# Unit outputs behind the next unit's chain: a recurrence in chunks feeding a routed MoE

## The chip, the cores and the metric

The kernel runs on one core of a Trainium2 chip. The metric is the device time of one execution in microseconds (us). Engines are named as in the profile: PE is the matrix engine (PEld its weight loads), DVE the vector engine, ACT the scalar engine, POOL GpSimd, SP the queue that issues most DMAs.

## The reference

```python
for t in range(S):                                  # S=768, B=4, H=8, D=40
    y[:, :, t] = einsum('bhd,bhde->bhe', r_t, state)
    Sa = einsum('bhde,bhe->bhd', state, a_t)
    state = state*w_t[:, :, None, :] - einsum('bhd,bhe->bhde', Sa, b_t) \
            + einsum('bhd,bhe->bhde', v_t, k_t)
x = y.transpose(0, 2, 1, 3).reshape(B*S, H*D)       # N=3072 tokens of 320
logits = x @ w_gate + log1p(exp(x @ w_noise)) * noise
# two largest logits of each token, softmax over the two -> top2, top2_w
out[mask_e] += top2_w * (relu(x @ w1[e]) @ w2[e])   # 8 experts, hidden 1024
```

A linear recurrence with a 40x40 state for each of 32 heads, and behind it a mixture of 8 experts of which every token takes two.

## The kernel before

**Units.** The sequence is cut into 12 chunks of 64 steps and the batches into two pairs, which gives 24 units n = 0 to 23; unit n works on chunk n//2 and pair n%2. Its chain needs the state that unit n-2 left (`Sst`, one per pair). Four units make a group; there are six groups.

**Preparing a group.** While group w runs, group w+2 is prepared. `prepA` makes the decayed factors (on DVE: the scan `Gx`, then `NH`, `raww`, `NG_`, `nge`, `rawba`, `gm`, `pk`), once per batch pair, behind the state updates of units 4w and 4w+2. They go to DRAM and come back as PE operands (`d_ab`, `st_ab`). `scoresL`, called in iterations 4w+1 and 4w+3, makes the scores: `psc<-st_ab` on PE (two blocks of 16 matmuls for one batch pair), `lt` and `lo` on ACT, `scr` to DRAM on SP. When both pairs are there, `tsolve` loads all of the group's triangles at once (`X<-scr` on SP, one buffer), solves them in 30 pairs of steps (`Tt<-X`, L582, and `X<-X,Tt`, L583) on DVE for groups 0 and 1 and on POOL for groups 2 to 5, and stores the result (`scr<-X`). `fetchB` brings it back for each unit as `T` (`T<-scr`, on POOL's queue).

**A unit.** Its pieces on PE: the *chain*: `pW<-sE` (state times operand), `pQ<-w,T` (first apply, 64 matmul rows in the trace), `pW<-q,lo`, `pQ<-w,T` again (second apply, 32 rows), then `pS`, which ends in DVE's new `Sst` (L686). PE and ACT alternate in it: `w<-pW` and `q<-pQ` are copies on ACT. *pre* makes the next unit's `psc<-st_ab,st_k`, `ak` on DVE and `pW<-Vz,ak`. *outp*, the output: `pu` turns `Ut` (copied to `uT` on DVE), two halves of `psc<-RV(,uT)` through a single PSUM buffer, each taken out by DVE as `P` (L699), `pd` turns the state (`sD`, one buffer), `pY<-sD,RV`, `pY<-kb,P`, `pgm`, and DVE's product `xt` (L709). *Logits*: `xd<-xt` to DRAM, `px<-idm,xt`, `xT`, `pl`, then some 40 short operations on DVE and ACT, and *placing* (`drain`, one unit later: the one-hots `ohA`, `ohB`, then `pn<-ohB,ohA`), which counts the tokens of each expert.

**Order.** The order on every engine is written out by the tile scheduler at build time, from the program's order and priorities: the chain has a high priority (`PRIO=1500`), everything else stands where the program puts it and moves up where its inputs and buffers allow. A matmul burst runs through the helper at L470 (transposes L471), so their line says nothing; the tile names do.

**Experts.** After the last unit the tokens are sorted, gathered and put through the experts (`ph` L287, `po` L309).

Of the kernel before, what the change touches and what calls it, by code (L numbers as in the profile page):

```python
# [8 lines left out]
F32 = mybir.dt.float32  # L9
# [11 lines left out]
NA=20  # L21
# [382 lines left out]
class Att:  # L404
    PSC=1; PACC=3; PT=2; PPB=1
    def __init__(s,nc,tc,ctx,aps):
        s.nc,s.tc,s.aps=nc,tc,aps
        ec=ctx.enter_context
        s.inp=ec(tc.tile_pool(name="inp",bufs=1))
        s.tmp=ec(tc.tile_pool(name="tmp",bufs=1))  # L410
        o=sorted(range(SAB),key=lambda i:(i-12)%SAB); s.sab={i:ec(tc.tile_pool(name=f"sab{i}",bufs=1)) for i in o}
        s.stk=ec(tc.tile_pool(name="stk",bufs=1))
        s.wk=ec(tc.tile_pool(name="wk",bufs=2))
        s.cp=ec(tc.tile_pool(name="cp",bufs=1))
        s.late=ec(tc.tile_pool(name="late",bufs=1))
        s.dr=ec(tc.tile_pool(name="dr",bufs=2,space=DRAM))
        s.psa=ec(tc.tile_pool(name="psa",bufs=1,space=PSUM)); s.psb=ec(tc.tile_pool(name="psb",bufs=1,space=PSUM)); s.ps=ec(tc.tile_pool(name="ps",bufs=1,space=PSUM))
        s.consts()
    def consts(s):
        nc=s.nc; t=s.cp.tile  # L420
        nc.scalar.preload_act_table_set("natural_log_exp_and_others")
        s.d1=t([120,NS,65],F16,name="d1"); nc.vector.memset(s.d1,0.0); nc.vector.memset(s.d1[:,:,0:1],1.0)
        s.idf=t([128,128],F32,name="idf"); nc.gpsimd.memset(s.idf,1.0)
        nc.gpsimd.affine_select(out=s.idf,in_=s.idf,pattern=[[1,128]],base=0,channel_multiplier=-1,compare_op=ALU.is_equal,fill=0.0)
        s.ids=t([128,128],F16,name="ids"); nc.vector.tensor_scalar_mul(s.ids,s.idf,SC)
# [172 lines left out]
    def fetchR(s,o,cc):  # L598

        nc=s.nc; n,p=o['n'],o['G']['p']  # L600
        vt=s.aps[1][p,cc]; o['vu']=s.stk.tile([128,2,8,40],F32,name="vu",bufs=VUB)
        nc.sync.dma_start(o['vu'][0:64].rearrange("p b h e->p b (h e)"),vt.rearrange("(b s) x->s b x",b=2))
        rv=s.RV[n%2]
        for j in range(2): nc.sync.dma_start(rv[64*j:64*j+48,j:j+2].rearrange("p x i b t->p (x i b t)"),s.aps[3][p,cc,j])
        o['v'],o['r'],o['rr']=rv[:,1],[rv[:,0],rv[:,2]],rv[:,0::2]
# [45 lines left out]
    def turned(s,p):  # L651

        pd=s.ps.tile([128,4,2,64],F32,name="pd",tag="pt",bufs=s.PT)
        s.burst([s.tp(pd[:,i].rearrange("p b e->p (b e)"),s.Sst[p][:,2*i:2*i+2].rearrange("p h d->p (h d)"),s.idf) for i in range(4)])
        sD=s.wk.tile([128,4,2,40],F32,name="sD",bufs=1)
        s.copy(ESD,sD,pd[...,0:40])
        return sD
    def chain(s,p,cc,o):
# [28 lines left out]
        return sD  # L687
    def outp(s,o,sD,xout):
        nc=s.nc; kb=o['kb']
# [5 lines left out]
        for b in range(2):  # L695
            pp=s.psa.tile([128,4,2,64],F32,name="psc",tag="psc",bufs=s.PSC)
            s.burst([s.mm(pp[64*j:64*j+64,i],x[:,i,b],o['rr'][:,:,i,b],start=True,stop=True) for i in range(4) for j,x in ((1,uT),(0,o['v']))])
            m=s.wk.tile([128,8,64],F32,name="P",bufs=2)
            nc.vector.tensor_tensor(m,pp.rearrange("p i j t->p (i j) t"),s.mk.to_broadcast([128,8,64]),op=ALU.mult)  # L699
            P.append(m)  # L700
        Y=s.psb.tile([128,8,64],F32,name="pY",tag="pacc",bufs=s.PACC)
        if sD is not None:
# [8 lines left out]
    def run(s,m,xo=None):  # L711
# [11 lines left out]
        def idx(n): g,q=divmod(n,4); c,p=divmod(q,2); return g,c,p,g*CG+c  # L723
# [3 lines left out]
        def fR(n):  # L727
            if n<N: s.fetchR(O[n],idx(n)[3])
        def O_(n): g,c,p,cc=idx(n); return O.get(n) or {'G':grp[g][p],'c':c}
        def fB(n):  # L730
# [5 lines left out]
        s.prepC(grp[0][0],gate)  # L736
        with after(s.sl.ins): fA(0); fR(0)
        s.prepC(grp[0][1],gate)
        with after(s.sl.ins): fA(1); fR(1)
        s.pre(O[0]); s.blocks(O[0])  # L740
# [3 lines left out]
        if m is not None:  # L744
            with after(xd),(ExitStack() if 0 in MG else after(pl)): m.consts2(s.dm.bitcast(F32))
        xts=[]; aD=None; rA,rC={},{}
        for n in range(N):
# [19 lines left out]
            if q%2 and (gn if q==1 else gn+1)<NG:  # L767
                z=(gn,1) if q==1 else (gn+1,0)
                with behind(n-1): rA[z]=s.loadA(z[1],z[0])
            aD=s.aD  # L770
            if n+1<N: s.pre(O[n+1])
            xt=s.wk.tile([128,360],F32,name="xt",bufs=2)
            s.outp(O[n],sD,xt); xt=xt[:,0:DM]
            if n+1<N: s.blocks(O[n+1])
            fA(n+2); fR(n+2)
            if m is not None:
                m.drain(1)
                if n==NA+1: m.drain(); m.turn()
                m.logits(2*cc+p,xt,s.ps,("pt","pp"),(s.PT,s.PPB))
                if ZN<=n<ZN+4:  # L780
                    with after(m.xw.ins): m.zero(n-ZN)
            else: nc.sync.dma_start(xo[p,cc],xt)
LA=7; LC=4; RB=3
# [19 lines left out]
ZN=12  # L803
# [98 lines left out]
def build(nc,tc,A,out):  # L902
    with ExitStack() as ctx:
        m=Moe(nc,tc,ctx,(A['wgn'],A['nz'],A['w1'],A['w2'],out))
        with ExitStack() as c2:
            s=Att(nc,tc,c2,(A['fm'],A['vt'],A['fm2'],A['rv']))
            m.burst=s.burst; s.run(m)
            m.flag(s.ps,"pt",s.PT,s.mags)
# [28 lines left out]
```

## Time and profile before

| | us |
|---|---|
| median of 3 runs | 997.6 (996.33 to 1008.94) |
| profiled execution | 1001.79, its span 999.9 |
| PE busy | 800.1 (80%) |
| DVE busy | 555.8 (56%) |
| ACT busy | 392.1 (39%) |
| POOL busy | 349.6 (35%) |

The span is what the trace shows of the profiled execution; the rest of its time lies around the span. All positions in the trace are microseconds from the span's start, and all rows come from this one execution. The units run from about 90 to 577 us, the experts from there to the end.

### The profile page before, as it was taken

The page shows a single profiled execution, that of the slowest core. Times are in us where ns is not written, and L with a number is a line of the kernel's source. Part 1 is how long each engine was busy: PE and PEld are TensorE (multiplying, and loading weights), DVE is VectorE, ACT ScalarE, POOL GpSimd, SP SyncE. Part 2 cuts the span into 40 slices and gives each one's busy share as a digit, 9 for nine tenths or more (in the row PEclk, how much of TensorE's full clock was granted, in tenths as well). Part 3 has the DMA queues.
Part 4 walks back from the last instruction along what each step waited for, and adds up shares of the span by engine and source line. Part 5 has one row for each costly group of instructions (what it writes and reads, how often), then busy time and mean ns, then how long its engine had stood idle before and what let it go on. Part 6 is the DMA issues. An engine that isn't in the chain of part 4 may idle for free.

```text
span 999.9 us, 27350 instructions
## 1 busy us (share of the span) xinstructions
PE 800.1 (80%) x11706; PEld 701.9 (70%) x11706; DVE 555.8 (56%) x1198; ACT 392.1 (39%) x820; POOL 349.6 (35%) x477
## 2 busy tenths in 40 slices
PE   0123556888885988898788689999999999999995
PEld 0113455767764767676667478899999999999995
DVE  9358658857489687447357471643444444443430
ACT  2202343355453355353335232543434444343421
POOL 6000000149449429629500105416060707070403
PEclk9999957697797999999988799999999999999998
DMA  4794888586785957973553204507070706161303
GB/s 117 188 230 111 223 216 219 138 232 156 185 251 123 239 154 189 270 197 91 140 159 118 69 8 86 171 13 195 7 195 8 191 11 187 16 178 25 37 7 40
DMA packets 102022, 134.72 MB, mean 135 GB/s; under 512 B 37232, under 2 KB 82996, under 8 KB 100852
## 3 DMA queue, kind: packets, MB, share of 16 engines
q1 hardware_dynamic: 90100, 110.60, 41.1%
q0 software_dynamic: 11792, 22.29, 11.1%
q8 instruction: 94, 1.54, 0.7%
q14 instruction: 36, 0.29, 0.1%
HBM read 96.25 MB, written 39.88 MB: 136 GB/s over the span
## 4 chain that ended last, share of the span: by engine, by line
PE 54%; DVE 13%; DMA 11%; POOL 9%; issue 6%; ACT 3%; SPq 2%; POOLq 0%; ACTq 0%; DVEq 0%
PE ph L287 19%; PE po L309 17%; POOL X L583 4%; POOL Tt L582 4%; PE psc L470 3%; PE pY L470 2%; PE pt L268 2%; PE pW L470 2%; DMA T<-scr 2%; DVE X L583 2%; PE pQ L470 2%; DVE Tt L582 2%; DMA X<-scr 2%; DMA d_ab<-pk 1%; DMA scr<-X 1%
## 5 line engine op out<-in xcount | busy, mean ns | idle before, releaser
L311 POOL DMA_INDIRECT out_dram<-y,oi x56 | 94.2, 1682 | 227.1 <-ACT y L310 214.9
L290 DVE SCALAR_TENSOR_TENSOR hl<-ph,hh 128x256 fp32r<-128x256 f32 (+1 forms) x128 | 71.1, 557 | 132.3 <-ACT hh L288 131.8
L288 ACT ACTIVATE hh<-ph 128x320 fp32r<-128x320 f32 (+1 forms) x128 | 66.0, 519 | 151.8 <-PE ph L287 150.4
L470 PE MATMUL pQ<-w,T 32*32 32x40 f32 x2304 | 44.4, 214 | 47.7 <-DMA T<-scr 33.8
L583 POOL TENSOR_TENSOR X<-X,Tt 128x30 f32<-128x30 f32 (+14 forms) x120 | 78.1, 651 | 8.8
L470 PEld LDWEIGHTS pQ<-w,T 32*32 32x32 f32 x2304 | 37.7, 119 | 58.4 <-issue 38.5
L252 POOL DMA_INDIRECT xr<-xd,gi x56 | 54.8, 979 | 61.7 <-DVE dv L177 28.2
L309 PE MATMUL po<-w2h,hh 128*128 128x320 f32 x384 | 74.2, 313 | 0.6 <-ACT hh L288 0.6
L582 POOL TENSOR_TENSOR Tt<-X 128x30 f32<-128x30 f32 (+14 forms) x120 | 71.5, 596 | 8.5
L309 PE MATMUL po<-w2h,hl 128*128 128x320 f32 x384 | 70.8, 311 | 0.0
L287 PE MATMUL ph<-xh,w1h 128*128 128x512 f32 (+1 forms) x256 | 69.4, 355 | 1.0 <-DVE hl L290 1.0
L287 PE MATMUL ph<-xh,w1l 128*128 128x512 f32 (+1 forms) x256 | 68.9, 350 | 0.0
L287 PE MATMUL ph<-xl,w1h 128*128 128x512 f32 (+1 forms) x256 | 68.6, 349 | 0.0
L699 DVE TENSOR_TENSOR P<-psc,mk 128x512 f32<-128x512 f32 x48 | 33.0, 687 | 63.3 <-PE psc L470 63.3
L470 PE MATMUL psc<-RV,uT 128*64 128x128 f32 x384 | 61.5, 309 | 7.0 <-DVE P L699 4.8
L309 PE MATMUL po<-w2l,hh 128*128 128x320 f32 x384 | 65.7, 309 | 0.0
L585 POOL DMA_DIRECT2D scr<-X x5 | 3.2, 648 | 173.7 <-DVE X L583 172.5
L309 PEld LDWEIGHTS po<-w2h,hh 128*128 128x128 f32 x384 | 61.0, 188 | 3.4 <-ACT hh L288 0.8
L470 PE MATMUL psc<-RV 128*64 128x128 f32 x384 | 61.5, 309 | 1.2 <-issue 1.1
L470 PEld LDWEIGHTS <-st_ab 120*64 120x64 f16 (+1 forms) x928 | 28.6, 122 | 45.1 <-issue 28.6
L309 PEld LDWEIGHTS po<-w2h,hl 128*128 128x128 f32 x384 | 59.8, 188 | 0.5
L470 PEld LDWEIGHTS psc<-RV,uT 128*64 128x64 f32 x384 | 47.8, 155 | 15.7 <-DVE P L699 6.5
(315 smaller groups left out, 1927.6 us busy)
## 6 DMA issues: line engine op xcount, KB each, us to landing
w2r<-in_w_dram SPq DMA_DIRECT2D x8, 1280.0 KB
RV<-in_rv_dram SPq DMA_DIRECT2D x48, 192.0 KB
rawba<-in_fm_dram SPq DMA_DIRECT2D x24, 360.0 KB
d_ab<-pk SPq DMA_DIRECT2D x24, 360.0 KB
st_ab<-d_ab SPq DMA_DIRECT2D x12, 720.0 KB
w1r<-in_w_dram SPq DMA_DIRECT2D x8, 1024.0 KB
raww<-in_fm_dram SPq DMA_DIRECT2D x12, 365.6 KB
st_ab<-d_ab SPq DMA_DIRECT2D x24, 180.0 KB
```

Source lines behind the costliest of these rows:

```text
L252: k=t//128; nc.gpsimd.indirect_dma_start(out=X[:p,k if s.cap==CAP else 0],out_offset=None,in_=s.xd[int(w is not s.early[0])],in_offset=OFF ...
L268: for t,p in tiles(t0,n): nc.tensor.transpose(pt[:,t-t0:t-t0+p],x[:p,t//128,f0:f0+128],s.idm[:p,:p])
L287: for i,(a,b) in enumerate(mm): nc.tensor.matmul(ph[:,:n],a,b,start=i==0,stop=i==7)
L288: nc.scalar.activation(hh[:,f,:n],ph[:,:n],AF.Relu)
L290: if c.stop>c.start: nc.vector.scalar_tensor_tensor(o,ph[:,c],0.0,hh[:,f,c].bitcast(F32),op0=ALU.max,op1=ALU.subtract)
L309: s.lm=nc.tensor.matmul(po[:p],h[:,f,r],w[:,f],start=k==0,stop=k==23); k+=1
L311: st=nc.gpsimd.indirect_dma_start(out=s.out_d,out_offset=OFFS(ap=idx[:p,e,ii:ii+1],axis=0),in_=y[:p],in_offset=None,compute_op=ALU.add)
L470: def mm(s,*a,**k): return lambda: s.nc.tensor.matmul(*a,**k)
L582: eng.tensor_tensor(t,Xt[:,j:j+1,j+1:].to_broadcast([128,j,m]),Xt[:,0:j,j:j+1].to_broadcast([128,j,m]),op=ALU.mult)
L583: s.tl=eng.tensor_tensor(Xt[:,0:j,j+1:],Xt[:,0:j,j+1:],t,op=ALU.add)
L585: q.dma_start(scr2.rearrange("g c h i j x->(g c h i) (j x)"),Xt.rearrange("p j t->p (j t)"))
L699: nc.vector.tensor_tensor(m,pp.rearrange("p i j t->p (i j) t"),s.mk.to_broadcast([128,8,64]),op=ALU.mult)
```

## The change

`outp` is cut in two. The new `outp` keeps `pu`, `uT`, the two `psc<-RV` halves and `P`; the rest (`pY`, `pgm`, `xt`) is `outq`. A new function `finish(n)` holds `outq`, the store of `xt`, the placing and the logits. In iteration n it is called for unit n-1, behind unit n's chain in program order, and once more after the loop. `sD` gets two buffers, since the turned state of unit n-1 is now read after unit n has written its own. The load of `RV` is taken out of `fetchR` into `fetchV` and issued for unit n+1 behind `finish(n-1)`, one iteration later than before. The recurrence takes the MoE's identity matrix `idm` in place of one of its own.

```diff
-    def __init__(s,nc,tc,ctx,aps):
-        s.nc,s.tc,s.aps=nc,tc,aps
+    def __init__(s,nc,tc,ctx,aps,idm):
+        s.nc,s.tc,s.aps,s.idf=nc,tc,aps,idm
...
-        s.idf=t([128,128],F32,name="idf"); nc.gpsimd.memset(s.idf,1.0)
-        nc.gpsimd.affine_select(out=s.idf,in_=s.idf,pattern=[[1,128]],base=0,channel_multiplier=-1,compare_op=ALU.is_equal,fill=0.0)
...
+    def fetchV(s,o,cc):
+        nc=s.nc; n,p=o['n'],o['G']['p']
         rv=s.RV[n%2]
         for j in range(2): nc.sync.dma_start(rv[64*j:64*j+48,j:j+2].rearrange("p x i b t->p (x i b t)"),s.aps[3][p,cc,j])
...
-        sD=s.wk.tile([128,4,2,40],F32,name="sD",bufs=1)
+        sD=s.wk.tile([128,4,2,40],F32,name="sD",bufs=2)
...
-    def outp(s,o,sD,xout):
+    def outp(s,o):
...
             P.append(m)
+        return P
+    def outq(s,o,P,sD,xout):
+        nc=s.nc; kb=o['kb']
         Y=s.psb.tile([128,8,64],F32,name="pY",tag="pacc",bufs=s.PACC)
...
+        def finish(n):
+            if n<0: return
+            g,c,p,cc=idx(n)
+            xt=s.wk.tile([128,360],F32,name="xt",bufs=2)
+            s.outq(O[n],*P.pop(n),xt); xt=xt[:,0:DM]
+            if m is None: nc.sync.dma_start(xo[p,cc],xt); return
+            m.drain(1)
+            if n==NA+1: m.drain(); m.turn()
+            m.logits(2*cc+p,xt,s.ps,("pt","pp"),(s.PT,s.PPB))
+            if ZN<=n<ZN+4:
+                with after(m.xw.ins): m.zero(n-ZN)
...
             aD=s.aD
+            finish(n-1)
             if n+1<N: s.pre(O[n+1])
-            xt=s.wk.tile([128,360],F32,name="xt",bufs=2)
-            s.outp(O[n],sD,xt); xt=xt[:,0:DM]
+            if n: fV(n+1)
+            P[n]=(s.outp(O[n]),sD)
             if n+1<N: s.blocks(O[n+1])
             fA(n+2); fR(n+2)
-            if m is not None:
-                m.drain(1)
-                if n==NA+1: m.drain(); m.turn()
-                m.logits(2*cc+p,xt,s.ps,("pt","pp"),(s.PT,s.PPB))
...
+        finish(N-1)
```

What this does to the written order shows at three places. The first is PE around unit 16, the first of group 4. Before: the output of unit 15, the first apply of unit 16 (`pQ<-w_6700,T`), then the scores of group 5's second batch pair in two blocks with the output halves of unit 15 between them, and `pY` after `P` within the same unit.

```order
L471 MATMUL pu<-idf,Ut 128x128 x4
...
L470 MATMUL pQ<-w_6700,T 32x40 x32
...
L470 MATMUL psc<-st_ab 64x64
L470 MATMUL psc<-RV_175,uT 64x128
...
L470 MATMUL pW<-q,lo 32x40 x16
...
L470 MATMUL psc<-RV_175 64x128
L470 MATMUL pQ<-w_6752,T 32x40 x16
...
L470 MATMUL pY<-kb,P 64x64 x12
```

The same place after; `pQ<-w_6185,T` is the second apply of unit 15, `pQ<-w_6543,T` the first of unit 16, and `pY` here belongs to unit 14.

```order
L468 MATMUL pQ<-w_6185,T 32x40 x16
L468 MATMUL pY<-sD,RV_171 64x64 x12
L468 MATMUL pY<-sD,RV_171 64x40 x4
L468 MATMUL pY<-kb,P 64x64 x12
L468 MATMUL pY<-kb,P 64x40 x4
L468 MATMUL pS<-vu,kb 40x40 x16
...
L468 MATMUL psc<-st_ab 64x64
L468 MATMUL pW<-Vz_169,ak 64x64 x12
...
L468 MATMUL pQ<-w_6543,T 32x40 x32
```

Both blocks of scores now stand ahead of unit 16's first apply (the second lies between the `pQ<-dm,idh` fillers and it), and `pY<-kb,P` no longer follows its own `P` within the unit. The same holds around units 4, 8 and 12.

The second place is ACT's queue at the end of unit 11, whose last copy `w<-pW` (`w_5187`, in the other kernel `w_5108`) is the one that unit 12's first apply waits for. Before:

```order
L676 ACTIVATE vu<-pQ 64x320
L98 ACTIVATE xT<-px 128x384
L678 ACTIVATE Ut<-pQ 128x8x40
L473 ACTIVATE sD<-pd 128x320
L473 ACTIVATE w_5187<-pW 128x320
L643 ACTIVATE sfs<-Sst_170 128x320
L105 ACTIVATE lg<-pl 128x16
L505 ACTIVATE raww<-Gx 120x768
L506 ACTIVATE raww<-raww 120x768
```

After:

```order
L678 ACTIVATE Ut<-pQ 128x8x40
L566 ACTIVATE lt<-psc 128x256
L566 ACTIVATE lo<-psc 128x256
L643 ACTIVATE sfs<-Sst_167 128x320
L503 ACTIVATE raww<-Gx 120x768
...
L504 ACTIVATE raww<-raww 120x768
L471 ACTIVATE w_5108<-pW 128x320
L649 ACTIVATE sE<-pst 120x320
```

`w` of unit 12 stood ahead of `sfs` and of the two `raww` of the next preparation and now stands behind them (and behind the second pair of `lt` and `lo`, left out here). Behind unit 9 the same happens to one `raww`; behind units 2, 4, 6, 8, 12 and 14 it is `pk<-rawk` that now stands ahead of the next unit's `w`, where it stood behind it.

The third place is SP's queue before the solve of group 2. Before: the scores go out, then one load of `RV`, one store of `d_ab` of group 3, and `X<-scr`.

```order
L570 DMA scr<-lo 32x16x32
L604 DMA RV_175<-in_rv_dram 48x1024 x2
L526 DMA d_ab<-pk 120x2x768
L575 DMA X<-scr 128x1024
L528 DMA d_ab<-pk 120x2x768
L491 DMA rawba<-in_fm_dram 120x768
L95 DMA xd_829<-xt 128x320
L532 DMA st_ab<-d_ab 40x3x768
```

After:

```order
L568 DMA scr<-lo 32x16x32
L95 DMA xd_826<-xt 128x320
L487 DMA raww<-in_fm_dram 120x780
L476 DMA st_k<-d_k 80x1152
L476 DMA st_k<-d_k 40x1152
L524 DMA d_ab<-pk 120x2x768
L526 DMA d_ab<-pk 120x2x768
L489 DMA rawba<-in_fm_dram 120x768 x2
L530 DMA st_ab<-d_ab 40x3x768
L529 DMA st_ab<-d_ab 80x4608
L530 DMA st_ab<-d_ab 40x3x768
L573 DMA X<-scr 128x1024
```

`X<-scr` of group 2 now stands behind the whole round trip of group 3's first factors (`d_ab` out, `st_ab` back). For groups 3 to 5 it still follows its four `scr` stores closely.

## Rows read from the trace of the kernel before

**Rows 1.** The page: its first line.

```profile
span 999.9 us, 27350 instructions
```

**Rows 2.** A window of 100 us: busy time of PE, PEld, DVE, ACT, POOL; clock, DMA share, GB/s.

```profile
700.00:800.00 100.00, 100.00 (x613) 93.18 (x612) 43.04 (x80) 41.72 (x75) 38.14 (x28) 1.00 0.39 100
```

**Rows 3.** Timeline of PE: first applies of units 8, 12, 16, 20; first expert matmuls.

```profile
271.66 0.79 PE L470 MATMUL pQ<-w,T 32*32 32x40 f32 x64
352.09 0.79 PE L470 MATMUL pQ<-w,T 32*32 32x40 f32 x64
427.25 1.29 PE L470 MATMUL pQ<-w,T 32*32 32x40 f32 x64 [2.56 <-DMA T<-scr]
496.53 1.29 PE L470 MATMUL pQ<-w,T 32*32 32x40 f32 x64 [5.89 <-DMA T<-scr]
577.46 1.66 PE L287 MATMUL ph<-xh,w1h 128*128 128x512 f32 x6
```

**Rows 4.** Timeline of the loops of groups 3, 4 and 5 on SP, POOL and PE.

```profile
282.47 1.36 SPq L575 DMA_DIRECT2D X<-scr  x1
343.08 3.53 POOL L608 DMA_DIRECT2D T<-scr  x4 [7.99 <-issue]
362.20 0.34 SPq L575 DMA_DIRECT2D X<-scr  x1
432.11 0.44 PE L470 MATMUL psc<-st_ab 120*64 120x64 f16 x16
437.31 0.34 SPq L575 DMA_DIRECT2D X<-scr  x1
489.89 3.53 POOL L608 DMA_DIRECT2D T<-scr  x4 [4.24 <-PE ptr L470]
```

**Rows 5.** Waits of PE, 190 to 580 us: total, times, longest.

```profile
PE pQ L470 <- DMA T<-scr: 9.2, 3, 5.9
PE px L97 <- DVE xt L709: 8.2, 4, 2.5
PE pQ L470 <- ACT w L473: 8.1, 2, 5.2
...
PE pY L470 <- DVE P L699: 4.4, 7, 0.9
```

**Rows 6.** Waits of PE's weight loads, 150 to 580 us.

```profile
PEld pY L470 <- DVE P L699: 9.3, 11, 1.3
```

**Rows 7.** Windows of PE alone: length, busy time, clock, DMA share, GB/s.

```profile
427.00:430.60 3.60, 3.35 (x92) 0.53 0.11 18
...
496.50:502.20 5.70, 5.67 (x108) 0.50 1.04 180
```

**Rows 8.** Groups of ACT instructions, 190 to 580 us: busy, mean ns, idle before.

```profile
L473 ACT ACTIVATE w<-pW 128x320 f32<-128x320 f32 x40 | 17.4, 436 | 19.7 <-PE pW L470 19.3
...
L459 ACT ACTIVATE pk<-rawk 120x768 f16<-120x768 f32 x6 | 5.1, 845 | 2.9 <-DVE rawk L399 2.6
L505 ACT ACTIVATE raww<-Gx 120x768 f32<-120x768 f32 x6 | 5.1, 845 | 7.0 <-DVE Gx L399 7.0
```

**Rows 9.** Windows of the solves of groups 3, 4 and 5 (columns as Rows 2).

```profile
288.00:334.50 46.50, 32.41 (x696) 26.11 (x696) 40.35 (x94) 17.62 (x41) 42.21 (x72) 0.82 0.73 189
366.80:413.50 46.70, 40.87 (x1056) 33.94 (x1054) 31.61 (x45) 24.13 (x55) 41.72 (x62) 0.94 0.80 214
443.40:485.10 41.70, 36.10 (x967) 29.98 (x969) 29.73 (x90) 18.48 (x47) 37.34 (x72) 1.00 0.41 121
```

**Rows 10.** Groups of DVE instructions, 120 to 560 us (columns as Rows 8).

```profile
L474 DVE COPY uT<-pu 128x512 f32<-128x512 f32 x22 | 15.1, 685 | 5.8 <-PE pu L471 5.7
...
L399 DVE TENSOR_TENSOR_SCAN Gx<-raww,d 120x780 f32<-120x780 f32 x7 | 13.1, 1869 | 0.0
```

**Rows 11.** Timeline of SP at the solve of group 2.

```profile
207.94 0.34 SPq L575 DMA_DIRECT2D X<-scr  x1
...
215.03 0.81 SPq L532 DMA_DIRECT2D st_ab<-d_ab  x1
```

More of the change, by code (lines that the diff above doesn't have):

```diff
@@ L728, in fR, with fV @@
             if n<N: s.fetchR(O[n],idx(n)[3])
+        def fV(n):
+            if n<N: s.fetchV(O[n],idx(n)[3])
         def O_(n): g,c,p,cc=idx(n); return O.get(n) or {'G':grp[g][p],'c':c}
@@ L736, in run @@
         s.prepC(grp[0][0],gate)
-        with after(s.sl.ins): fA(0); fR(0)
+        with after(s.sl.ins): fA(0); fR(0); fV(0)
         s.prepC(grp[0][1],gate)
-        with after(s.sl.ins): fA(1); fR(1)
+        with after(s.sl.ins): fA(1); fR(1); fV(1)
         s.pre(O[0]); s.blocks(O[0])
@@ L745, in run @@
             with after(xd),(ExitStack() if 0 in MG else after(pl)): m.consts2(s.dm.bitcast(F32))
-        xts=[]; aD=None; rA,rC={},{}
+        aD=None; rA,rC={},{}; P={}
+        def finish(n):
[9 more added lines that the diff above has]
+                with after(m.xw.ins): m.zero(n-ZN)
         for n in range(N):
@@ L770, in run @@
             aD=s.aD
+            finish(n-1)
             if n+1<N: s.pre(O[n+1])
-            xt=s.wk.tile([128,360],F32,name="xt",bufs=2)
-            s.outp(O[n],sD,xt); xt=xt[:,0:DM]
+            if n: fV(n+1)
+            P[n]=(s.outp(O[n]),sD)
             if n+1<N: s.blocks(O[n+1])
             fA(n+2); fR(n+2)
-            if m is not None:
-                m.drain(1)
-                if n==NA+1: m.drain(); m.turn()
-                m.logits(2*cc+p,xt,s.ps,("pt","pp"),(s.PT,s.PPB))
-                if ZN<=n<ZN+4:
-                    with after(m.xw.ins): m.zero(n-ZN)
-            else: nc.sync.dma_start(xo[p,cc],xt)
+        finish(N-1)
 LA=7; LC=4; RB=3
@@ L905, in build @@
         with ExitStack() as c2:
-            s=Att(nc,tc,c2,(A['fm'],A['vt'],A['fm2'],A['rv']))
+            s=Att(nc,tc,c2,(A['fm'],A['vt'],A['fm2'],A['rv']),m.idm)
             m.burst=s.burst; s.run(m)
```

## The prediction

> **What bounds the kernel now.** Read the windows first. From 600 us on PE is full [rows 2]: the experts run there, the change does not touch them, and whatever it does has to move the start of the experts, at 577.46 [rows 3]. So the stretch of the units is read alone.
>
> In it I read the first applies of every fourth unit, since one group's `T` serves four units [rows 3]. From unit 8 to unit 20 they stand at 271.66, 352.09, 427.25 and 496.53: 80.4, 75.2 and 69.3 us per group, 224.9 together. Two of them wait for the load of `T`, 2.56 and 5.89 us [rows 3], and these make most of the 9.2 us that PE waits for it at all [rows 5].
>
> Why `T` is late shows in the loop [rows 4]. `X` of group 5 is loaded at 437.31, 10.1 us behind unit 16's first apply, because the last block of its scores runs only at 432.11, behind that apply, and `X` follows the scores by 5.2. From there to the apply that needs the solution it takes 496.53 - 437.31 = 59.2 us. For group 4 the same two pieces are 10.1 and 427.25 - 362.20 = 65.1. For group 3 `X` goes out 10.8 behind unit 8's apply; `T` is issued at 343.08, and with the 6.6 us from issue to apply that unit 20 shows (496.53 - 489.89) it is there 67.2 after `X`; unit 12 starts 2.4 later than that. So two loops out of three are closed by the solve, the third by PE's own work. The waits list names the other losses: `pY` for `P` and `px` for `xt`, both outputs of the running unit that PE asks for too soon, and `pQ` for ACT's `w` [rows 5].
>
> A wait also costs afterwards: the first apply takes 0.79 us for unit 12 and 1.29 for units 16 and 20 [rows 3], and the granted clock is 0.53 for 3.6 us and 0.50 for 5.7 us there, 1.2 of 2.4 GHz [rows 7].
>
> **The change part by part.**
>
> *The scores come before the apply.* With the output of unit n-1 behind chain n, both blocks of group 5's second pair stand ahead of unit 16's first apply, and likewise at units 8 and 12. If the last block ends about as the apply starts (it takes 0.44 and fillers follow it, so I set it 1 us ahead), `X` goes out 5.2 - 1 = 4.2 us behind the apply where it was 10.1: each loop is 5.9 shorter. That covers the 2.56 and just the 5.89: -8.4. What follows them at half clock, 9.3 us, is work that at full clock takes half of it, so at most 4.6 more; I take -4, since the short gaps that remain may keep some of it.
>
> A ceiling for this part: the three loops would become 67.2 + 4.2, 65.1 + 4.2 and 59.2 + 4.2, 204.1 together, against 224.9. No saving of PE between units 8 and 20 can give more than 20.8 as long as the solve takes what it takes.
>
> *`P` and `xt` are ready when they are asked for.* `pY<-kb,P` of unit n-1 now stands far behind its `P`. The wait is 4.4 us in PE's own list and 9.3 in that of the weight loads, over a longer stretch [rows 5, 6]; the two overlap, I take the middle: -7. `px<-xt` loses 8.2 [rows 5]; in the new order it stands well behind `xt` at odd units, and at even ones as close as before. Half of it: -4.
>
> *The price on ACT.* By the new order `w`, which the first apply needs, stands behind a `pk<-rawk` or a `raww` in eight places where it stood ahead of it (the second place shown with the change). Each is 0.85 us long and waits itself for DVE's work behind the new state [rows 8]. Bounds for the eight: the 0.44 of one copy each where PE has other work to do meanwhile, 3.5 [rows 8], and 8.1/2 = 4.05 each, which is what the two such waits of this trace cost [rows 5], 32.4. What is queued behind the waiting copy is `sE`, for the unit after next, which is not urgent; who waits for it is PE, with everything behind the first apply. I take 1 us each, 8, near the lower end, because in most of the eight `px` and `pW<-Vz,ak` stand ahead of that apply on PE anyway.
>
> *The first groups.* The solve of group 1 runs on DVE. By the order another set of instructions now stands inside it: one scan more (1.87), two `uT` more (1.37) [rows 10] and shorter ones, less a few `rawk` and `pk`, which I estimate at 7 us in all. Group 2's `X<-scr`, which went out at 207.94, now stands behind the `st_ab` loads of group 3, the last of which went out at 215.03, 7.1 later [rows 11]. Against it stands that its scores, too, come before the apply, and that those `st_ab` need a preparation which DVE now does earlier, inside the solve. Bounds: 5.9 gained, as in the other loops, and 7 + 7.1 = 14.1 lost. I take +2.
>
> *The rest costs nothing.* The second `sD` only keeps the two units' turned states apart. Two instructions on POOL at the start go. The `RV` loads are issued about a unit later, but what reads them (`outp`) has not moved ahead; cover is the unit between, some 15 us (a quarter of the 59 to 67 above). If that were gone, the load's latency would show in front of `psc<-RV` once per unit. The last unit's output still stands ahead of the experts.
>
> The sum is -8.4 - 4 - 7 - 4 + 8 + 2 = -13.4. The profiled execution took 1001.8 (its span 999.9 [rows 1]), 4.2 over the median of 997.6, so 988.4 by the profile is **984 us** by the median. That is 1.4%; this kernel's measurement can tell about 2% from no change.
>
> **The rivals.**
>
> *The loop was the only bound, and it opens everywhere: 967 us.* The ceiling of 20.8 is reached, the first groups gain 5.9 and the units behind 496 lose their share of the waits for `P` and `xt`, say 4: -30.7, 1001.8 - 30.7 - 4.2 = 966.9. For it: two loops of three end in a wait for `T`. Against it: PE itself took 2.4 us longer than the third loop, so it has to shed work or waits there too.
>
> *The solve stretches, and the loop closes again: 989 us.* The three solves took 46.5, 46.7 and 41.7 us, the short one where the group's preparation has ended [rows 9]. With DVE's and SP's work packed closer to it, each loop could be as long as the longest: 3 x (67.2 + 4.2) = 214.2, 10.7 less than now. That takes the place of all that PE could gain between units 8 and 20; the last units still give some 4 for `P` and `xt`, ACT's price counts half, because the loop hides the rest, and the first groups stay at 2: -10.7 - 4 + 4 + 2 = -8.7, 1001.8 - 8.7 - 4.2 = 988.9. Against it: the second solve had DVE busy for 31.6 of 46.7 us and the first for 40.4 of 46.5, and both were equally slow [rows 9]; it is not DVE's busy share that sets it. The Trainium skill, "GPSIMD Engine Reference", section 1 (Specifications), says that GpSimd shares its SBUF interfaces with VectorE and contends with instructions that have two SBUF inputs or run in a 2-port mode. The rows bear this out only in part, for the reason just given; by that rule this rival would be the likelier one, since the logits' one-hots and the preparation now crowd into the same stretches.
>
> *ACT's queue becomes the bound, and it is slower: 1009 us.* All eight places cost what the two known ones do, 32.4 in place of 8: -13.4 + 24.4 = +11, 1012.8 - 4.2 = 1008.6. Its point of decision is a wait of (13.4 + 8)/8 = 2.7 us per place; above it the change loses. For it: the queue is in order, one such wait reached 5.2 [rows 5], and behind unit 11 four instructions of the preparation and the scores now stand ahead of `w`. Against it: at units 12 and 16 the loop leaves room for a late `w`.
>
> **How the numbers follow.** Forecast 0.42, the open loop 0.22, the closed loop 0.21, ACT 0.15. The forecast's own range is 972 to 996, from its bounds (ACT 3.5 to 16, the first groups -6 to +10). The range that should hold 8 in 10 reaches below the open loop and stops short of ACT's full price: 962 to 1004. Faster by over 2% is below 977.6: nearly all of the open loop, and about a quarter of the forecast, 0.33. Slower by over 2% is above 1017.6: two fifths of ACT's case, 0.06. Within 2%: 0.61.
>
> **What would show it.** In the trace of the changed kernel: no wait for `T` at units 16 and 20, and `X<-scr` about 4 us behind the first applies of units 8, 12 and 16 (right); waits of `pY` for `P` gone and of `px` halved; `pQ` for `w` in more places than two, but around 1 us each. The forecast is wrong if `X` still follows by 10, if the solves last well over 47 us, if `pQ` waits for `w` by more than 2.7 us a time, or if unit 8 starts later than 282.

## The result and the profile after

The changed kernel takes 1017.0 us, the median of four runs (1011.97 to 1019.99), the kernel before 1002.64 in the four runs beside them (996.33 to 1008.94): a ratio (changed to before) of 1.0134, 95% interval 1.0094 to 1.0174. The forecast was 984 with a range of 962 to 1004, against the 997.6 known then, a ratio of 0.986. It is slower where a gain was forecast.

The first lines to read are the same first applies as in [rows 3], on PE's timeline of the changed kernel, with unit 4 ahead of them and the first expert matmuls at the end.

```profile
212.90 1.29 PE L468 MATMUL pQ<-w,T 32*32 32x40 f32 x64 [10.94 <-DMA T<-scr]
278.41 0.79 PE L468 MATMUL pQ<-w,T 32*32 32x40 f32 x64 [0.45 <-ACT w L471]
361.59 1.03 PE L468 MATMUL pQ<-w,T 32*32 32x40 f32 x64
440.30 0.77 PE L468 MATMUL pQ<-w,T 32*32 32x40 f32 x62
509.46 1.29 PE L468 MATMUL pQ<-w,T 32*32 32x40 f32 x64 [3.56 <-DMA T<-scr]
587.54 0.94 PE L287 MATMUL ph<-xh,w1h 128*128 128x512 f32 x3
```

Unit 4 in the kernel before:

```profile
197.41 0.78 PE L470 MATMUL pQ<-w,T 32*32 32x40 f32 x64 [0.75 <-DMA T<-scr]
```

Unit 4 starts 15.5 us later, unit 8 6.7, unit 12 9.5, unit 16 13.1, unit 20 12.9, the experts 10.1. The span grew by 10.3, so the experts themselves are unchanged. In this trace the loss has two places: the first groups, and the units 8 to 16.

The loops, on SP's and POOL's timeline (answering to [rows 4]):

```profile
284.17 0.34 SPq L573 DMA_DIRECT2D X<-scr  x1
340.92 2.65 POOL L608 DMA_DIRECT2D T<-scr  x3 [3.46 <-PE px L97]
362.65 0.34 SPq L573 DMA_DIRECT2D X<-scr  x1
418.77 2.65 POOL L608 DMA_DIRECT2D T<-scr  x3 [4.05 <-DMA scr<-X]
445.76 0.33 SPq L573 DMA_DIRECT2D X<-scr  x1
454.33 2.13 POOL L574 TENSOR_TENSOR X<-X,tri 128x1024 f32<-128x1024 f32 x1 [19.32 <-DMA X<-scr]
494.76 0.60 POOL L583 DMA_DIRECT2D scr<-X  x1 [0.31 <-POOL X L581]
500.45 3.52 POOL L608 DMA_DIRECT2D T<-scr  x4 [5.09 <-PE pQ L468]
```

`X<-scr` now follows the first applies of units 8, 12 and 16 by 5.8, 1.1 and 5.5 us; it was 10.8, 10.1 and 10.1. `T` of group 4 is issued 21.5 us ahead of the apply that needs it: the loops of groups 3 and 4 did open, and PE arrived later anyway. The loop of group 5 closed again. `X` leaves 4.6 us closer behind unit 16's apply, but from there to unit 20's apply it takes 63.7 us instead of 59.2: from the load of `X` to the mask (`X<-X,tri`) 8.6 instead of 6.1, the solve 40.4 instead of 41.6, from its end to the issue of `T` 5.7 instead of 4.8, and from that to the apply 9.0 instead of 6.6. So unit 20 follows unit 16 by 69.2 us, as it did before (69.3), with a wait for `T` in both.

The waits of PE from 190 to 580 us, as in [rows 5], then two lines of the same view of the kernel before, and the one weight-load line that answers to [rows 6]:

```profile
PE pQ L468 <- DMA T<-scr: 14.5, 2, 10.9
...
PE pW L468 <- DVE ak L621: 7.4, 4, 3.0
PE pst L468 <- DVE sfs L644: 7.0, 7, 2.5
PE pQ L468 <- ACT w L471: 6.9, 12, 2.4
PE px L97 <- DVE xt L712: 4.9, 3, 2.4
...
PE pd L469 <- ACT kb L471: 4.1, 4, 1.3
```

```profile
PE pW L470 <- DVE ak L621: 0.7, 1, 0.7
...
PE pst L470 <- DVE sfs L644: 0.2, 1, 0.2
```

```profile
PEld pY L468 <- DVE P L699: 2.2, 3, 1.1
```

What was to go went: at units 16 and 20 3.6 us of waiting for `T` are left of 8.4, the weight loads of `pY` wait 2.2 us for `P` instead of 9.3, `px` 4.9 instead of 8.2 (in the weight loads' list of the same stretch it hardly fell, 8.9 instead of 9.6). But 10.9 us of `T` are new, at unit 4, and `ak`, `sfs` (the new state, split for `sE`) and `kb` (the copies on ACT of the operands that `pY` and `pS` read) took the place of the rest: 7.4, 7.0 and 4.1 us, where before there were 0.7, 0.2 and none. By group of units, in windows of the kernel before (length, PE, PEld, DVE, ACT, POOL busy, clock, DMA share, GB/s) from unit 8 on:

```profile
271.70:352.10 80.40, 63.46 (x1574) 51.67 (x1573) 66.12 (x142) 36.75 (x88) 46.45 (x76) 0.89 0.76 195
352.10:427.20 75.10, 61.74 (x1567) 51.10 (x1566) 48.42 (x73) 36.10 (x83) 45.86 (x67) 0.93 0.77 205
427.20:496.50 69.30, 57.75 (x1544) 48.43 (x1544) 39.04 (x111) 29.94 (x77) 41.43 (x76) 0.97 0.49 140
496.50:577.50 81.00, 63.95 (x1408) 52.22 (x1408) 46.98 (x150) 31.12 (x77) 5.73 (x12) 0.84 0.41 114
```

and of the changed one:

```profile
278.40:361.60 83.20, 63.70 (x1574) 54.45 (x1574) 63.19 (x137) 38.81 (x92) 48.03 (x76) 0.88 0.76 189
361.60:440.30 78.70, 64.37 (x1567) 53.94 (x1566) 47.84 (x77) 33.76 (x78) 46.91 (x67) 0.84 0.69 181
440.30:509.50 69.20, 57.48 (x1501) 49.07 (x1503) 42.64 (x113) 28.93 (x74) 40.27 (x76) 0.95 0.58 157
509.50:587.50 78.00, 65.94 (x1473) 55.34 (x1474) 47.66 (x151) 33.65 (x82) 5.76 (x12) 0.83 0.42 122
```

Units 8 to 16 take 161.9 us instead of 155.5; of the 6.4, 2.9 are PE's busy time (at a clock of 0.84 instead of 0.93 in the second window, so the same work lasts longer) and 3.5 idle. From unit 20 on 3.0 are won.

**The start.** How unit 4 came to be 15.5 us late can be followed back from its `T`. In the kernel before, rows of ACT, SP, DVE and POOL, from the copies of group 1's last scores to the load of `T`:

```profile
129.45 0.38 ACT L568 ACTIVATE lt<-psc 128x256 f32<-128x256 f32 x1 [0.40 <-PE psc L470]
131.33 0.34 SPq L570 DMA_DIRECT2D scr<-lt  x1
139.89 0.55 SPq L575 DMA_DIRECT2D X<-scr  x1
147.44 1.22 DVE L576 TENSOR_TENSOR X<-X,tri 128x1024 f32<-128x1024 f32 x1
189.08 0.83 POOL L585 DMA_DIRECT2D scr<-X  x1 [172.46 <-DVE X L583]
193.25 3.61 POOL L608 DMA_DIRECT2D T<-scr  x4 [3.34 <-PE pW L470]
```

The same after the change:

```profile
130.49 0.64 PE L468 MATMUL psc<-st_ab 120*64 120x64 f16 x16
136.12 1.03 DVE L554 TENSOR_TENSOR rawk<-rawk,NH 120x384 f32<-120x384 f32 x2 [8.60 <-DMA rawk<-in_fm_dram]
137.18 0.84 ACT L457 ACTIVATE pk<-rawk 120x768 f16<-120x768 f32 x1 [6.46 <-DVE rawk L554]
137.93 0.36 ACT L566 ACTIVATE lt<-psc 128x256 f32<-128x256 f32 x1
138.32 0.33 SPq L568 DMA_DIRECT2D scr<-lt  x1
147.01 0.36 SPq L573 DMA_DIRECT2D X<-scr  x1
152.22 1.22 DVE L574 TENSOR_TENSOR X<-X,tri 128x1024 f32<-128x1024 f32 x1
198.62 0.83 POOL L583 DMA_DIRECT2D scr<-X  x1 [182.41 <-DMA d_ab<-pk]
205.41 3.61 POOL L608 DMA_DIRECT2D T<-scr  x4 [5.96 <-issue]
```

The scores are there at about 131, 1.7 us later than before, and their copy `lt` stands behind a `pk<-rawk` on ACT, which waits 6.5 us for DVE's `rawk`, and that waits 8.6 for its load: `scr` goes out 7.0 later and `X` is loaded 7.1 later. The mask (`X<-X,tri`) begins 4.8 later, the solve takes 46.4 us instead of 41.6, another 4.8, and the issue of `T` behind it 6.8 instead of 4.2. That makes 12.2 at `T`; with 7.5 us instead of 4.2 from the issue of `T` to the apply it is 15.5 at unit 4. Why the load of `rawk` came late was not followed further.

### The profile page after: what moved, and what is told of

It reads as the page before. It is cut to its first block, busy times and chain, and to the rows that moved or that the text cites. A ratio compares the mean times of both kernels' runs of the same rounds, so it can differ in the third digit from the quotient of the medians.

```text
span 1010.2 us, 27402 instructions
## 1 busy us (share of the span) xinstructions
PE 796.4 (79%) x11706; PEld 706.8 (70%) x11706; DVE 554.2 (55%) x1198; ACT 391.7 (39%) x820; POOL 349.9 (35%) x475
## 3 DMA queue, kind: packets, MB, share of 16 engines
q1 hardware_dynamic: 90100, 110.60, 41.1%
## 4 chain that ended last, share of the span: by engine, by line
PE 54%; DVE 10%; issue 5%; POOL 4%; DMA 4%; ACT 3%; SPq 0%; POOLq 0%; DVEq 0%; ACTq 0%
PE ph L287 18%; PE po L309 17%; PE psc L468 3%; PE pY L468 3%; PE pt L268 2%; PE pW L468 2%; PE pQ L468 2%; POOL X L581 2%; DMA T<-scr 2%; POOL Tt L580 2%; PE pS L468 1%; PE po L301 1%; PE po L300 1%; DVE Gx L399 1%; DMA X<-scr 1%
## 5 line engine op out<-in xcount | busy, mean ns | idle before, releaser
L288 ACT ACTIVATE hh<-ph 128x320 fp32r<-128x320 f32 (+1 forms) x128 | 65.8, 518 | 151.5 <-PE ph L287 150.1
L581 POOL TENSOR_TENSOR X<-X,Tt 128x30 f32<-128x30 f32 (+14 forms) x120 | 75.5, 629 | 8.6
L468 PE MATMUL psc<-RV,uT 128*64 128x128 f32 x384 | 63.7, 318 | 4.7 <-DVE uT L472 3.3
L468 PE MATMUL psc<-RV 128*64 128x128 f32 x384 | 63.7, 318 | 0.0
L309 PEld LDWEIGHTS po<-w2l,hh 128*128 128x128 f32 x384 | 58.6, 188 | 0.1
L468 PEld LDWEIGHTS psc<-RV,uT 128*64 128x64 f32 x384 | 49.8, 160 | 10.3 <-DVE uT L472 4.0
```

Of the source, the lines that this page charges most:

```text
L288: nc.scalar.activation(hh[:,f,:n],ph[:,:n],AF.Relu)
L309: s.lm=nc.tensor.matmul(po[:p],h[:,f,r],w[:,f],start=k==0,stop=k==23); k+=1
L468: def mm(s,*a,**k): return lambda: s.nc.tensor.matmul(*a,**k)
L581: s.tl=eng.tensor_tensor(Xt[:,0:j,j+1:],Xt[:,0:j,j+1:],t,op=ALU.add)
```

## The experiments

All are compared with the kernel before, run beside them on the same chip. In the edits `fin1(n)` is `outq` of unit n and `fin2(n)` its placing and logits; a run "late from 7" puts both behind the next chain for units 7 and up.

**First reading: `finish(n-1)` stands ahead of `pre(n+1)`.** The waits list suggests it, and a stretch of unit 13's start does. On DVE `xt`, the one-hots of the placing and then `ak`, for which PE stands still:

```profile
380.23 0.49 DVE L712 TENSOR_TENSOR xt<-pY,xt 128x320 f32<-128x320 f32 x1 [0.25 <-issue]
...
381.38 1.06 DVE L162 TENSOR_TENSOR ohB<-ohD,vals 128x512 f16<-128x512 f16 x1
...
383.06 1.07 DVE L162 TENSOR_TENSOR ohB<-ohD,vals 128x512 f16<-128x512 f16 x1
...
384.05 0.68 DVE L621 TENSOR_TENSOR ak<-psc,mk 128x512 f32<-128x512 f32 x1
...
384.78 1.13 PE L468 MATMUL pW<-Vz,ak 128*64 128x64 f32 x32 [2.43 <-DVE ak L621]
```

```diff
-            finish(n-1)
             if n+1<N: s.pre(O[n+1])
+            finish(n-1)
             if n: fV(n+1)
```

> The changed kernel with the next unit's pre (psc<-st_ab,st_k, ak, pW<-Vz,ak) put ahead of finish(n-1) in the program instead of behind it. Theory A: the change loses because finish(n-1) stands between chain n and pre(n+1), so that on DVE xt, xT and the placing's one-hots stand ahead of ak, on which the next first apply hangs; then the wait of pW for ak (9.3 us in 5 times after the change) falls under 3 us, the units 8 to 16 take 156 us or less instead of 162, and the time is 1005 to 1010 against 1017. Rival B: ak is only where an idle that comes from elsewhere (clock, start, ACT) shows; then the waits move to other names and the time stays at 1014 to 1020.

Ratio 1.0186 (1.0101 to 1.0272): nothing is won; theory A's 1005 to 1010, a ratio of 1.002 to 1.007, is not reached.

```diff
-            finish(n-1)
             if n+1<N: s.pre(O[n+1])
-            if n: fV(n+1)
             P[n]=(s.outp(O[n]),sD)
+            finish(n-1)
+            if n: fV(n+1)
```

> The changed kernel with finish(n-1) at the end of iteration n, behind pre(n+1) and outp(n). Theory A: as in the run with pre first, and the two P of unit n come ahead of the output of unit n-1 as well, 1003 to 1010; pY waits for P no more than 5 us. Rival B: 1014 to 1020. Rival C (the later the output, the more it crowds the next unit): 1020 or more.

Ratio 1.0232 (1.0156 to 1.0308), rather slower than the change itself. Here the wait did go: from 270 to 450 us PE waits for `ak` 0.6 us in two times. The time did not follow, so theory A fell; rival C's 1020 or more, a ratio of 1.017, fits.

**Which units lose it.** A first pair of runs divided the units at 7, with `finish(n)` right behind `outp(n)` for the units that are not late:

```diff
-            finish(n-1)
+            late=lambda k: k>=7            # the other run: k<7
+            if n and late(n-1): finish(n-1)
             if n+1<N: s.pre(O[n+1])
             if n: fV(n+1)
             P[n]=(s.outp(O[n]),sD)
+            if not late(n): finish(n)
             if n+1<N: s.blocks(O[n+1])
```

> Outputs of units 0 to 6 are finished in their own iteration, as before the change; from unit 7 on they stand behind the next chain, as after it. Theory S (the start): unit 8 starts at 278.4 instead of 271.7 because the order of the first units' work lengthens the first solve and delays the first groups, and this alone is some 7 of the 10 us between the two traces; then unit 8 starts at 271 to 273 and the time is 1008 to 1011. Rival L: the later units lose it (8 to 16: 162 us instead of 156), the early part is made up by the slack of T; then the time stays at 1014 to 1018.

> The mirror image: outputs of units 0 to 6 stand behind the next chain, from unit 7 on they are finished in their own iteration. Theory S: unit 8 starts at about 278 and the time is 1008 to 1011, 6 to 8 over the kernel before. Rival L: the time is that of the kernel before, 1000 to 1005, since T's loop takes up the late start.

1.0236 (1.0160 to 1.0312) and 1.0264 (1.0178 to 1.0349): both halves come out worse than the whole. The division was not clean: in the kernel before, placing and logits stand behind `blocks(n+1)` and the loads of the next units, and here they stood ahead of them for the units that should have been as before. The next runs keep that place, and the `RV` load too; for units that are not late the written order is then that of the kernel before.

```diff
+            if n and late(n-1): fin1(n-1); fin2(n-1); fV(n+1)
             if n+1<N: s.pre(O[n+1])
             P[n]=(s.outp(O[n]),sD)
+            if not late(n): fin1(n)
             if n+1<N: s.blocks(O[n+1])
             fA(n+2); fR(n+2)
+            if not late(n): fV(n+2); fin2(n)
```

With `late` false for all units, and `fV(n+1)` behind `pre(n+1)` as in the change, only the small parts are left:

> The kernel before with all of the change but its point: the MoE's identity, two sD, and RV of unit n+1 loaded in iteration n behind pre(n+1); output, placing and logits stay in their own iteration. The written order of PE, DVE and ACT is that of the kernel before, on SP nine transfers stand a place or two later. Theory N: these parts cost nothing, ratio 0.997 to 1.003. Rival R: an RV load that waits for the last reader of its buffer holds up SP's queue behind it, 3 to 8 us more (ratio 1.003 to 1.008), with psc<-RV waiting for RV.

Ratio 0.9983 (0.9958 to 1.0009). Identity, second `sD` and the later `RV` load cost nothing. The run also shows how well positions repeat: its first applies of units 4 to 20 and its first expert matmul stand within 1.2 us of those of the kernel before.

> The output, placing and logits of units 0 to 6 stay where the kernel before has them (placing and logits behind blocks(n+1) and the loads, which the earlier run of this split did not keep), from unit 7 on they stand behind the next chain. Theory S (the start): the changed kernel's unit 8 starts 6.7 us late because of the first groups; without them 3 to 4 us of the loss remain, ratio about 1.004. Rival L (later groups): they alone lose it, ratio 1.010 or more. In the trace unit 8 should start at 270 to 274.

Ratio 0.9996 (0.9971 to 1.0022), unit 8 at 273.1. No loss is left, where theory S expected about 1.004.

> The mirror image: units 0 to 6 late, from unit 7 on everything where the kernel before has it. Theory S: unit 8 starts at about 278, ratio 1.006 to 1.010. Rival L: ratio 1.000 to 1.004, the late start is taken up by T's loop.

Ratio 1.0154 (1.0106 to 1.0202), unit 4 at 214.3, unit 8 at 283.5. The whole net loss is that of the early units, more than theory S gave them.

**What in the early units.** The written order lets one choose: with unit 0 as before, `lt` and `lo` of group 1 come ahead of `pk<-rawk` on ACT again, but still more work stands inside the solve; with units 0 and 1 as before, neither is disturbed.

> Only unit 0's output, placing and logits stay where the kernel before has them, all later ones stand behind the next chain. In the written order lt and lo of group 1's last scores stand ahead of pk<-rawk on ACT again, as before the change, but on DVE about 34 us of other work stand inside the first solve against 20 before and 27 after the change. Theory V (the solve on DVE is stretched by what stands inside it): X<-scr of group 1 at 140 to 142, as before, the solve from its mask to scr<-X 52 us or more, unit 4 at 207 to 213, ratio 1.008 to 1.016. Rival Q (what counts is X's late load, because lt and lo stand behind pk on ACT and RV holds up SP): with X on time unit 4 starts at 197 to 202 and the ratio is 0.996 to 1.004.

> Units 0 and 1 stay, from unit 2 on output, placing and logits are late. The written order has 20 us of other DVE work inside the first solve and lt and lo ahead of pk<-rawk, as before the change. Theories V and Q alike: the start is as before (X at 140 to 142, unit 4 at 197 to 201) and the ratio 0.995 to 1.003: the whole loss hangs on units 0 and 1. Rival G (the first solve is not it, the later early groups are): ratio 1.008 or more.

Late from 1: ratio 1.0124 (1.0085 to 1.0163); `X` on time at 141.1, and unit 4 yet later, at 217.6. Rival Q fell, and theory V held for the solve (54.4 us) and the ratio; unit 4 is later than its 207 to 213, because the issue of `T` follows the solve by 10.2 us instead of 4.2, for which the profile names no reason. Late from 2: unit 4 at 200.1 as forecast, ratio 1.0067 (1.0033 to 1.0102), over the 1.003 that V and Q allowed: the start is mended, and half the loss stays. Rival G's early groups are not where it lies in this trace: unit 8 is 2.7 us late, unit 12 2.9, unit 16 9.6. The first applies of unit 4 on PE's timeline, late from 1 and late from 2 (there the window shows 52 of the 64 rows):

```profile
217.63 1.29 PE L468 MATMUL pQ<-w,T 32*32 32x40 f32 x64 [10.95 <-DMA T<-scr]
```

```profile
200.13 1.09 PE L468 MATMUL pQ<-w,T 32*32 32x40 f32 x52
```

The solve's length by what stands inside it: windows of DVE from the mask to `scr<-X` (length, busy, clock, DMA share, GB/s). The kernel before, the changed one, late from 1:

```profile
147.44:189.08 41.64, 37.13 (x92) 0.62 0.72 178
```

```profile
152.22:198.62 46.40, 42.80 (x102) 0.76 0.71 177
```

```profile
148.84:203.27 54.43, 48.52 (x110) 0.68 0.61 167
```

The solve's own 60 steps are busy 19.8, 19.7 and 19.7 us in these windows. The other work is then 17.3, 23.1 and 28.8 us, and the solve takes 41.6, 46.4 and 54.4: per microsecond of other work about one more (5.8 gives 4.8, 11.5 gives 12.8). The order on DVE is written at build time, so it is not the length of the window that lets the work in. Late from 2 (17.0 of other work) takes 40.9.

```diff
-TPOOL=(2,3,4,5)
+TPOOL=(1,2,3,4,5)
```

> The changed kernel with group 1's solve on POOL as well. Theory V: other DVE work no longer lengthens it; X still comes at about 147, the solve takes 42 to 47 on POOL, scr<-X at 195 to 200 and unit 4 at 209 to 213: little is won there, but DVE is free for the first units, ratio 1.005 to 1.013. Rival Q: as the load of X is late either way, the same as after the change, 1.011 to 1.017. If it is under 1.003, the stretch on DVE was most of the loss.

Ratio 1.0105 (1.0069 to 1.0140), `X` at 146.8, the solve 44.7 us on POOL, unit 4 at 208.2. The interval overlaps that of the change and reaches into both forecasts, so a gain is not shown and V and Q are not told apart; with `X` still late the stretch cannot be bought off on POOL, which is hardly faster (44.7 us there, 46.4 on DVE).

**Placing and logits without the output.**

```diff
+            if n: fin2(n-1)
             if n+1<N: s.pre(O[n+1])
             P[n]=(s.outp(O[n]),sD); fin1(n)
             if n+1<N: s.blocks(O[n+1])
             fA(n+2); fR(n+2); fV(n+2)
-            fin2(n)
```

> Only placing and logits of unit n-1 stand behind chain n, the output (pY, pgm, xt) stays in its own iteration. Theory D (short DVE and ACT work ahead of ak and kb of the next unit is what costs): the loss is there without the late output, ratio 1.010 to 1.020, with pW waiting for ak and pd for kb. Rival O (the late output is what costs, by pY and its xt ahead of the next unit's work): ratio 1.000 to 1.005.

Ratio 0.9939 (0.9911 to 0.9967): this half of the change gains, so theory D fell; rival O is left, though the gain is outside its range, and the late output alone was not run. It gains although the solve is longer here too (45.4 us with 21.4 of other work) and unit 4 starts at 204.5, 7.1 us late; at unit 8 0.3 of that is left. With units 0 and 1 left as they were:

> The output stays in its own iteration; only placing and logits stand behind the next chain, from unit 2 on, so that the first solve has 20 us of other work in it instead of 25 in the run with all of them late. Theory V: unit 4 starts at 197 to 200 instead of 204.5, and this adds to that run's gain: ratio 0.986 to 0.994. Rival P (PE's own path is what sets the later units, a lead at unit 4 is waited off by unit 8): 0.993 to 1.000.

Ratio 0.9912 (0.9880 to 0.9944), unit 4 at 199.0, in theory V's range. That mending the start adds to the gain is not shown: the two intervals overlap, and of the 5.5 us that unit 4 is ahead of the run before 1.0 is left at unit 8, as rival P has it. Here what the forecast expected of the whole change does in part happen. Units 16 and 20 and the load of `X` behind unit 16, on PE and SP:

```profile
425.74 0.26 PE L468 MATMUL pQ<-w,T 32*32 32x40 f32 x5 [0.17 <-DMA T<-scr]
490.63 0.49 PE L468 MATMUL pQ<-w,T 32*32 32x40 f32 x32
```

```profile
431.12 0.34 SPq L573 DMA_DIRECT2D X<-scr  x1
```

The last scores of group 5 start at 422.5, ahead of unit 16's apply; `X` follows the apply by 5.4 us instead of 10.1, the profile names no wait for `T` at unit 20, and from unit 16 to unit 20 it takes 64.9 us instead of 69.3. Both applies break off, though, after the 5 and the 32 rows shown, for 2.0 and 2.9 us, without a releaser that the profile could name.

**Early, middle, end.** The four runs of this part were made on a chip where the kernel before takes 1015.9 us (median); the experts take 429 to 432 us in them, 422 in the trace of the kernel before. Their ratios are against that kernel on that chip, and their positions are read against each other: late from 15 has the order of the kernel before up to unit 14, late for 7 to 14 has it from unit 15 on.

> Output, placing and logits late from unit 15 on only, where no group is prepared any more. Theory M (the late output collides with the preparation on DVE in the middle and gains behind it): units 8 to 16 take 154 to 157 us as in the kernel before, from unit 16 to the experts 143 to 146 instead of 150, ratio 0.992 to 0.996. Rival U (the last units gain nothing of their own either): 0.998 to 1.003.

> Late only for units 7 to 14. Theory M: units 8 to 16 take 158 to 162 us, ratio 1.002 to 1.007. Rival U: 0.997 to 1.002.

Late from 15: 0.9969 (0.9936 to 1.0003), units 8 to 16 in 157.1 us; from unit 16 to the experts it took 149.1, not the 143 to 146 of theory M, and 151.5 in the run that is late for 7 to 14 only. The gain there is small and not quite clear of noise, since its interval takes in 1. Late for 7 to 14 only: 1.0071 (1.0037 to 1.0104), units 8 to 16 in 164.0 us instead of 157.1. The middle loses, as M said.

> Late from unit 7 on, but pre(n+1) stands ahead of the late output, placing and logits in program order, so that ak does not stand behind xt and the one-hots on DVE. Theory K (ak's place is the loss in the middle): pW waits for ak less than 1 us a group and the ratio falls from 0.9996 to 0.993 or less. Rival (the wait only moves on): 0.997 to 1.005.

```diff
-            if n and late(n-1): fin1(n-1); fin2(n-1); fV(n+1)
             if n+1<N: s.pre(O[n+1])
+            if n and late(n-1): fin1(n-1); fV(n+1); fin2(n-1)
```

Ratio 1.0122 (1.0074 to 1.0170), worse than without (0.9996). PE waits for `ak` 6.1 us in seven times between units 8 and 16, not less than late from 7 has there (4.0 in four), and `px` and `pl` wait longer, up to 4.9 us at a time. So theory K's gain did not come, but its condition, that the wait goes, was not met either. What speaks against it is the run with `finish` last: there the wait went (0.6 us) and the ratio was 1.0232, though PE then waited for `P` (5.1 us in the same stretch).

> Placing and logits late from unit 2 on, the output late from unit 15 on. Theory M: the gains of late placing (0.991) and of the late output at the end add, ratio 0.984 to 0.990. Rival P (both gains are the same idle of PE in the last units): 0.989 to 0.994.

```diff
+            tl=lambda k: k>=2              # late is k>=15
+            if n and late(n-1): fin1(n-1); fV(n+1)
+            if n and tl(n-1): fin2(n-1)
             if n+1<N: s.pre(O[n+1])
```

Ratio 0.9847 (0.9798 to 0.9896), in theory M's range; the product of the two gains is 0.988 (0.9912 x 0.9969), and the interval just reaches rival P's 0.989. This version beats both kernels, the changed one by some 3% (1.0134/0.9847).

First applies of every fourth unit and the experts' start in the profiles (us), with the ratios; the rows marked * are from the chip of this last part:

| | 4 | 8 | 12 | 16 | 20 | experts | ratio |
|---|---|---|---|---|---|---|---|
| before | 197.4 | 271.7 | 352.1 | 427.2 | 496.5 | 577.5 | 1 |
| all late (the change) | 212.9 | 278.4 | 361.6 | 440.3 | 509.5 | 587.5 | 1.0134 |
| late to 6 | 214.3 | 283.5 | 364.8 | 440.1 | 508.3 | 588.2 | 1.0154 |
| late from 1 | 217.6 | 283.0 | 358.4 | 442.3 | 508.6 | 586.5 | 1.0124 |
| late from 2 | 200.1 | 274.3 | 355.0 | 436.9 | 506.9 | 580.8 | 1.0067 |
| late from 7 | 199.2 | 273.1 | 351.4 | 431.2 | 503.1 | 576.3 | 0.9996 |
| late from 15 * | 198.6 | 271.5 | 354.6 | 428.6 | 496.5 | 577.7 | 0.9969 |
| late 7 to 14 * | 199.2 | 272.4 | 351.5 | 436.4 | 499.7 | 587.9 | 1.0071 |
| placing, logits late from 2 | 199.0 | 271.0 | 351.8 | 425.7 | 490.6 | 569.5 | 0.9912 |

## Why the prediction was wrong, by its own steps

Two steps failed. The first groups stood in the sum at +2 and cost some 15 us: 1.0154 of some 1002 us, with units 0 to 6 alone late. The four gains stood at -23.4, less ACT's price of 8 at -15.4, and came out at about nothing: 0.9996, with units 7 to 23 alone late.

**The first groups** are the step that failed most. They stood in the sum at +2, with a bound of 14.1 above; by the trace unit 4 is 15.5 us late, unit 8 6.7. The two mechanisms were the right kind and one was named: other DVE work inside the first solve, estimated at 7 us and measured at 5.8, lengthens it nearly one for one (4.8 us). The other was priced on the wrong transfer: not group 2's `X` moved (it left at 204.89 instead of 207.94, for all the `st_ab` loads ahead of it), but group 1's, 7.1 late, because its scores' copy stood behind a waiting `pk<-rawk` on ACT (1.7 of it is the scores' own). With unit 0 as before, that order is gone and `X` is on time. The prediction had looked at ACT's queue only for `w`. Against it I set an earlier preparation of group 3 as a gain, with no row that showed it was needed earlier. The runs put the whole net loss on units 0 to 6. How it divides between the late `X` and the longer solve isn't separated by a run: with `X` on time and the solve longer still (late from 1) the loss was the same. Nor are these two all of it: with both mended (late from 2) 1.0067 stays, by the trace lost mostly between units 12 and 16.

**Scores before the apply (-8.4, and -4 for the clock).** The mechanism was right: `X` went out closer behind the first applies, by 5.8, 1.1 and 5.5 us (that their average of 4.1 meets the forecast of 4.2 is luck), and 4.9 of the 8.4 us of waiting for `T` at units 16 and 20 went. The gain did not follow. I took two of the three loops as closed by the solve and PE as free to use what was opened; but PE's own path through the units was as long, and it became longer: 231.1 us from unit 8 to unit 20 instead of 224.9, with `T` ready well ahead at unit 16. And I took the rest of each loop as it was, 59.2 us for group 5; it took 63.7, since the loads of `X` and `T` took longer, and that loop gave nothing. The rival of the loop that opens everywhere (967 us) fell with it. The clock gave nothing back either: 0.88, 0.84 and 0.95 in the three windows instead of 0.89, 0.93 and 0.97. At unit 16, where no wait for `T` is left, the first apply takes 0.77 us (62 of its 64 rows) instead of 1.29, so there the half clock went; at unit 20 it takes 1.29 as before.

**`P` and `xt` (-7 and -4).** The waits went almost as forecast by the lists that the forecast used, the first by 7.1 us in that of the weight loads (3.5 in PE's own), the second by 3.3 of 8.2 (0.7 of 9.6 in that of the weight loads). Their time did not come back: PE then waited for `ak`, `sfs` and `kb`, products of DVE or ACT. Of these `ak` was seen behind the late output and placing, at unit 13; `sfs` follows its state on DVE about as closely as before (by 1.0 to 2.8 us, one time 3.8; before by 1.0 to 3.7), so it was not displaced. The step that failed is taking a wait that goes as a time that is won, on an engine that waits for three others in turn. It also counted time twice: by the prediction's own ceiling group 5's loop could give 5.9 us, and the wait for `T` had taken all of it, so nothing was left there for `P` and `xt` to win.

**ACT's price for `w` (+8)** was about right per place, 0.6 us in 12 places where 1 in 8 was forecast. As a term of the sum it was too high: the two long waits of before (8.1) are gone, so by PE's list the total of 6.9 is 1.2 less than before. The rival of 2.7 us and more per place fell; the longest is 2.4.

**The rest at nothing** held: 0.9983 for the small parts. The rival in which the solve on POOL stretches found little: from mask to `scr<-X` groups 2 to 5 took 44.8, 48.2, 47.7 and 40.4 us, where the rows of before had 46.5, 46.7 and 41.7 for the last three, at most 1.7 more; what closed group 5's loop again were the loads. The Trainium skill, "GPSIMD Engine Reference", section 1 (Specifications), states that GpSimd contends with VectorE's instructions of two SBUF inputs. The case gives that no test: DVE was busy beside the last three solves for 41.1, 32.2 and 29.5 us, about as before (40.4, 31.6 and 29.7).

**What stays open.** Why the late output loses in the middle (1.0071 for units 7 to 14) is shown only by place: it loses while groups are prepared on DVE and not at the end. The wait for `ak` alone isn't it, by the run with `finish` last; the output was never made late in the middle without placing and logits. That the sequence of DVE's work as a whole is too full there is argued, not shown. The late placing and logits alone bring the scores ahead of the apply as well and leave the rest of the unit's order as it was; there the 8.4 us of waits for `T` at units 16 and 20 are down to 0.2, with 4.9 us of unnamed breaks in the same two applies; how much of their 0.9% this is, is not shown.

## What to carry to other kernels

Work that is moved behind a critical step of the next unit lands in another stretch; look there for a serial job on the same engine, since every microsecond of strangers inside it lengthened this one by about one. A wait that disappears is worth its time only if the engine has nothing else to wait for soon after; here some 12 us of waits for `T` (units 16 and 20), `P` and `xt` went from PE's list and others took their place. Such a move is best divided before it is judged: by stretch of the program and by part. Placing and logits of this one gained 0.6% (0.9% from unit 2 on), with the output added it lost 1.3%, and the two where each pays gained 1.5%.

## What had not been expected of the hardware

A solve of 60 dependent steps that are busy for 19.8 us takes 41.6 us on DVE with 17.3 of other work in it, and 44.7 on POOL with nothing else of DVE's inside (the run with the first solve moved): the move frees DVE and doesn't shorten the solve. And an in-order queue can carry a delay to a job that shares nothing with its cause: the load of group 1's triangles was late by 7.1 us, 1.7 of it by its scores, the rest behind a `pk<-rawk` on ACT whose load of `rawk` neither it nor its scores use.
